# Two decays of a recurrent state moved to VectorE, a matmul narrowed, and a new instruction order in a fused RWKV-6 and hard-swish kernel

## The chip, the cores and the metric

The kernel runs on one core of a Trainium2 chip. The metric is the device time of one execution in microseconds, as the median of several runs. The engines are named as the profile names them: PE is TensorE (PEld its weight loads), DVE is VectorE, ACT is ScalarE, POOL is GpSimd, SP is the engine whose queue issues nearly all transfers.

## What is computed

A recurrence over 768 steps for 4 sequences and 8 heads of width 48, then a feed-forward layer on its output, all in float32:

```python
for t in range(S):                                   # r, k, v, w: (4, 8, 768, 48); u: (8, 48)
    cur = einsum('bhd,bhe->bhde', u[None] * kt, vt)
    y[:, :, t] = einsum('bhd,bhde->bhe', rt, state + cur)
    state = wt[:, :, :, None] * state + einsum('bhd,bhe->bhde', kt, vt)
x = y.transpose(0, 2, 1, 3).reshape(3072, 384)
h = x @ w_in                                         # (384, 2048)
g = h * clip(h + 3, 0, 6) / 6
out = g @ w_out                                      # (2048, 384)
```

## The kernel before

The 3072 tokens are cut into 24 chunks of 128, six per sequence, and two sequences are worked in turn. Chunk `i` goes through these steps. `load_feat` brings its r, k and w. `back_scan` (L430, L434) and `fore_scan` (L439) are products of the decays over half a chunk, backward and forward, on DVE. `make_k` (L450) and `make_r` (L454) scale k and r with them, on DVE for the first seven chunks (`EARLY = 7`) and on POOL after that. `own` (L466, L467, on POOL from chunk 9) and `own_sum` (L483, DVE) give the term with u. `score` (L500) multiplies scaled k by scaled r on PE, and `above` (L507, DVE) copies the part above the diagonal out of PSUM, which frees two PSUM banks. `turn_k` (L516) transposes k, `write` (L600) forms what the chunk adds to the state, and `written` (L611, ACT) copies that out. The state is then carried on by four steps of one small instruction each, on tiles of 112x192 numbers: `decay` (L529: old state times the decay of the first half chunk), `middle` (L537: plus what that half adds), `decay_middle` (L529: times the decay of the second half), `new_state` (L545: plus what the second half adds). Both decays go through the helper `decayed`, so both have line L529; they run on DVE up to chunk 6 and on POOL from chunk 7 on. `read_state` (L578) and `read_values` (L587) give the chunk's output, and `leave` (L685, ACT) copies it to the tile `xT` that feeds the feed-forward layer. A sixth of the rows of `xT` is moved into place by `last_pair` (L692), transfers from SBUF to SBUF of three issues each on SP's queue, four of them for a block.

From chunk 4 on, the PE work of a chunk is one step, `read(i)`: read the state, a short matmul `mark` (L622), `score(i+1)`, another `mark`, `write(i+1)`, read the values, `turn_k(i+2)`. The matmuls of 64 or fewer rows and columns in it use a quarter of the array each, and four of them run at a time; the mark uses one quarter.

Four chunks make a block of 512 tokens; there are six. Block 0 takes the layer in the plain way (L718 up, L729 gate on DVE, L737 down). Blocks 1 to 5 take it by sums and fewer products: DVE first forms sums of the parts of x (`sum_x`, called tx, L780 to L784, written to the tile `T_`), PE runs 40 up products (L833) that leave 7 chains of sums in PSUM banks, DVE and ACT read these out (L850, L848, L841), ACT clips (L854), DVE multiplies (L858, the gate) and forms sums of gated values (`sum_g`, L873), and PE runs 28 down steps of eight products (L888), which ACT and DVE take out (L906, L908). Sums of the weights (`sum_w`, `sum_out`) are made once on DVE by the same lines L780 to L784 and L809. DVE also converts the weights at the start (L413, L417) and later reads inputs a second time to test their range (`vet`, L936 and L943).

One table sets the order of everything. Each step is added to a `Plan` with its engine, a cost in microseconds, the steps that it needs and the buffers that it holds. The string `ORDER` gives the rank of every step, two characters each; the steps are emitted in that rank, and each engine executes its own share of that sequence strictly in that order. The costs of the steps don't change this order when the program is built. They serve the search that made the string, which is not part of the kernel, and they set where `emit` puts idle products (`spin`, L1269) on PE in the first 60 us.

```python
rank = [CODE.index(ORDER[2 * i]) * 64 + CODE.index(ORDER[2 * i + 1]) for i in range(len(steps))]
```

Of the kernel before, what the change touches and what calls it, by code (L numbers as in the profile page):

```python
# [8 lines left out]
F32 = mybir.dt.float32  # L9
# [12 lines left out]
HL = L // 2  # L22
# [59 lines left out]
    "AAADAHAQAKAOAMANAPARASAYAWAjAUAXAaAeAmAqAgAoAzA3A/ACAFATAiAbAnAdAZAcAfAhAlAuAyAkApAxA1A5A9A8A+BOBUBeAJALBGBfBRBZBSBD"  # L82
    "BJBTBVBYCGCLBoBwCBCRBbCYCfCnCwC7AVAwBiB4BuCABzBdBgBlBmBqCSCaCJCOCWCrCNCuC1E1DBDMDVDfBPBQCpC3DdDkCvCUCbCiDDDXDuDyC+DG"
    "DiFCDLFGFKFcFZFnCXDKC9DHEPEbDCDADQDWDsEKFgDZDqFmE6FsFvF+FzF/HgHLCcC4D+EJFpFtEDDYDwD9FfFlF8FkGFF9GVGfGiGlGsDoGSETFjGD"
    "GJEXEEFJFRF6GLG0GBGoGbGvG4HBG+HHHSHVEdF2FwF7GpG1FyGHGIGWGtGzHYGqHPG9HUHcH2HtH4FxG5F1GUGwHEHaGrGQGYHQHjH5HIINHkITIYIw"
    "I4JHL3KhGOHJGRHCHlH0H6HZGkHXH+IOJIIDKPJzK/LELJLbHKKIHOHoIqJCJEIPHmH8KxKyLOKzLKKtLXLeLmL8MHMIHbLTHhJTJeLVLdJZIJIbLULa"
    "LxLgLsL0MNL9MtJLJfJOJtLRLqLzKOJ4LFLuL+MQLtMaNANnOYOeQBOqK3L2LCLiL1MFMJLrLMMBMDMiOkNhObM/OzO4PJPVPgLfOpL4MAMyOZOsMnM9"
    "NIO1PFPeOcPiPBPmPoQJPyP2QTQZM5PcM6NdOrPbPfNpNQOCPkPrP+PlQNPsQPQUQWQcQxNtOlNuPXPqP9QAPhO5PIQIQOQlP1QsQqRSRVR/R2TPTzUG"
    "OwQjOxPxQVQrQuP0PSQRQwRySGRBSSRdSsS2ThTsUJQkTZQ+Q2RRSFSvQ/RURmS5TOT0TQTwToT1UDUPUMUQUoUTRbSQRcSLTnT8UBS7RtSNT5UKUhT9"
    "UXUEUZUkU/U2WYSATySCTqTvUSUjTrTaTuUnU0U6UmVaUlVrXGXfXnXsYIYETYURTxUOUpVOVzUWUyU+XQXmXwVMXpVyXuXzX3YAVQVRVUVeWHXqXvVh"  # L90
    "VxW5XtX1X/XyX4X6X+YDYKYNYRYSBCABAEArAvAsA2AGA4A7AtBAAIBEBIA6BNBBB1B9B7CFCDClCoCmCyA0CTCZBrChBLCHCKCQC6CVC0C5DNDSD7Eh"
    "ElEgEsDPDzD2D1EcCgD/EBDREmCsDgDjDpDvEoE/FDE+FMEHErEuExE4E0FSFVFPFeDtE2E5EpFABHBMBWB3B8B/EUEaEiBaBhBtBjBxB0GCGZGaBcBk"
    "BpBnCCCPEAEIELBFBKBXBsByB2EFEOESB6CECIEeEnEvBvB5B+EwFTFXCMCdCjEMEREWCeCtCzEQEVEYC2C/DEFBFUFhC8DJDOEjEtEzCkCxDFD0D6EC"
    "CqDbDhEZEfEkDIDUDaGEGGGNDTDeDmE3E9FEDlDxD3EqEyE7DcDnDrD4EGENE8FIFNFWFiFqFrFuGAKYF5GKGPGTGXGcGhGnGuJPGxGyG2G6HAHFHGHN"
    "HRI+HTHdHfHiHpHrHxHzIHKuD5D8FFFHFLFOFQFYFbFdFoF3GMGdGgGjGmG3G7G/HDHMHWHeHnHqHuHwH1H3H/IBIEIKIUIXIeIiIlIvI0I6FaF0F4Ge"
    "G8IxJcLAHsHvICIVISIcIsI2JGIdIkItIQIRIhHyIIIFH9IaIpJAI3JDIWIfIZH7IyILIjIrIMIGI7IzIgImIuJFI/JKJUJ5KDJNJlI5I9IoI1JmJuJo"
    "JxJBJSInI8JRJgJyKAKbJrJ/KNJWJiJ2JJJVJhJQJbJpJ7JvKBJaJnJ0JMJ+JqJwKLJYJXKTKcJkJ8JsKEJ1KKKeKfKmKGKQKlKpKFKHKaKiKMKSKRKW"
    "J6J9KjK6KsK7KqLIK2K9KJKrKoKwLpLyK1K5K8LBLDLNLSLYK0K4K+MCLGLPLcMgLoLHLlLWLjLLLkLnL/KCKULQLhKgKkLZLwL6MLMEMGMRMVKZLvL7"
    "KnMTMMMeNvMjMPMSMUMlMkMsM3NMNaM1M+NPMoM0NFMWMcMqMXMuM4NLNGNRMmMxM2MYNEMwM7NHMfMpNSNUMzNVNCNNNJNWNsNwN0NKNON+N/NiNyNf"
    "NgN9ODNbNqNDNXNZNrOIOROgN4N8OKNzN2OBNYNlNkNTNmOHOaOQOhNjN5N6NeOLN3N7OENxNcOTONN1OFOJOiOVOmOtO0O3OdOjOfO2OOOSOUOXOuOv"  # L100
    "OPOWOAOGOMPWPAPLO7PMPHPPOnO8OyPCPTQFPGPNPQPRPaPdPpPtPEPKPOQgPUPnPuRCSBPYP6P3QKPZP4P5QCOoO6PjPvO+O/P7P/QQQbQLQMQaQnO9"
    "QDQEPDQhQSQvSESDQeQmQ3Q7Q0RDRLRWR6RERJRQQyRFRXQiQzQ5Q1RNRgRuR0SHQ8RHRPQtRORIRKRMQ6RARsRaRYReRqRxR5SISMSmSpR+SORhRkR4"
    "R7R3R8SaSjRTRrSTSYSKSWShStS0SdSlTESJSVSfRfRoRlRnRwR9SgSUSqSRSZSXRiSoRpSbS/RzRvSwTGR1SkSPSuSeSxS+TFTLSnSrTNTRSzS3S6TA"
    "S4S8TDTHScSiTBTMTTTfTSTiTcTjSyTUTKTWUaUdTbTeTgTlTmT3UAUCTXTdTkUzTpT6ULWBUxTtT+T7UIT2UiUNUgS1S9T4T/TITJUHUUUfUrUcUqUt"
    "U5TCUeUVTVU1UsVBWCVVUwU3U9VIVJVXVoV4WNWgWkWtVTVWVgU4U8VEVDVKVcV0VmV5VLVZVdU7VwVNV8WpVCVFWIXAVPVpViV2VqV7WrW1W7WRWTXB"
    "XHVvWKW0W9V/WGXCXIVjVsV1WFWVWbWhWoWuXSV+WEWWVGVfVYVnV3V9WMWLWfWAWPWJVSWXVbWSW8VkVuWcXWV6WdWDWZWQWiWjXJXLWmWsXZXbWwWx"
    "XNXUWnWqXOXTWOWUX2X9YJYPX5YQYLYVXKXgX8YBXkXxYMYOYTYYYWYXYaYeXiYCYUX0YfYZYjYlYmWeXMW6XcWyW4W/XVWlW2WvW+XFXXXDXEXoXrXY"
    "XaXhXjW3XPXRXdX7XeXlYGYHYFYnYbYcYhY3YkYuY6ZEZUYpY1Y/ZgZqZ2YdYoYvYgYtY4ZFY+ZKYsYxZyYiZBYyYzY2YrYqZJZCYwaQY8ZIZAZNZXZa"
    "ZoZGZQZTZWaXaZZYZjZsZzY7ZHaHaNY0Y9ZMZZZuZeZhZ0Z+aBaSZLZbZVZOZfZpZvZwZ6Y5ZDaKZPZRZcZiZnZdZSZkZ5ZlabZrZ7Z1Z9Z/aCaEaDaO"
    "Z8aAaeapZmZxaRaYZ3Z4aiarZtaJaIacaLavaaahaGaMaFaTaUadaVafagakama0a/bDaPaWalajaqa8bIanbKbTbLaoa7awa5axa6a4bCatauasaza1"  # L110
    "a3a2a+bEbJbFbGbNbPaybAbBa9bObHbQbMbRbSbUIAJdKdKvJjJ3KVKXMZMdL5MKMOMbMrM8NBNoMhMvPwPzP8QHQXQfQGQYQdQoQpQ9Q4RZRGRjUuVA"
    "UFUYUbUvVHVlVtWaWzbV"
# [132 lines left out]
def fast_path(tc, feat, tok, wflat, ub, ug, moe_w_in, moe_w_out, out, flag, n_chunks):  # L245
# [22 lines left out]
    with ExitStack() as ctx:  # L268
# [175 lines left out]
        def early(i):  # L444
            return nc.vector if i < EARLY else nc.gpsimd
# [85 lines left out]
        def decay(i):  # L531
            new_S(i)
            decayed(early(i), i, 0, states[i % 2])
# [87 lines left out]
        def mark():  # L621
            nc.tensor.matmul(pp.tile([HL, HL], F32, name="ps"), lhsT=ident[HL:, HL:], rhs=ident[HL:, HL:], start=True, stop=True)  # L622
# [378 lines left out]
        for i in range(NT):  # L1001
# [12 lines left out]
            plan.add(f"back{i}", "DVE", 1.40, do(back_scan, i), [f"feat{i}"] + [f"fore{i - 2}"] * (i > 1) + [f"back{i - 1}"] * (i > 0), k,  # L1014
                     [("E", [f"K{i}", f"least{i}"])], port=True)
            plan.add(f"K{i}", "DVE" if dve else "POOL", 0.59 if dve else 1.15, do(make_k, i), [f"back{i}", f"least{i}"] + [f"K{i - 1}"] * (i > 0) + ["later"] * (i == 0),
# [3 lines left out]
            plan.add(f"R{i}", "DVE" if dve else "POOL", 0.6 if dve else 1.15, do(make_r, i), [f"fore{i}"], k + 0.3,  # L1020
                     port=True)
            plan.add(f"least{i}", "ACT", 0.12, do(least, i), [f"back{i}"], k + 0.2)
            if i < BY_PE:
                plan.add(f"own{i}", "DVE", 0.6, do(own, i), [f"feat{i}"] + ["later"] * (i == 0) + [f"own{i - 1}"] * (i > 0), k + OWN,
                         [("rk", [f"dot{i}"])], port=True)
                plan.add(f"dot{i}", "PE", 0.56, do(own_dot, i), [f"own{i}"], k + OWN, [("ps", [f"sum{i}"])])
                plan.add(f"sum{i}", "ACT", 0.12, do(own_sum, i), [f"dot{i}"], k + OWN, [("dg", [f"diag1{i}"])])
            else:
                plan.add(f"own{i}", "POOL", 2.2, do(own, i), [f"rkt{i}", "u"] + [f"own{i - 1}"] * (i > 0), k + 0.4,
                         [("rk", [f"sum{i}"])], port=True)  # L1030
                plan.add(f"sum{i}", "DVE", 0.45, do(own_sum, i), [f"own{i}"], k + 0.5, [("dg", [f"diag1{i}"])])
# [26 lines left out]
            if not last:  # L1058
                plan.add(f"state{i}", "DVE", 0.27, do(new_state, i), [f"decb{i}"] + [f"decay{j}" for j in (i - 2,) if j >= 0 and not is_first(j)],
                         t + 0.5, port=True)  # L1060
# [15 lines left out]
            else:  # L1076
                uses = [f"up{bk}.{d}.{r}" for d in range(2) for r in range(20) if X_PLACE[r][0] == "w"] + [f"tx{bk}.{x}" for x in range(4)]
                space = [("x", uses)] * (c == 0)
                needs, us = [f"decb{i}", f"above{i}"], 1.24
# [33 lines left out]
        for f in range(NFC):  # L1113
            for c0, c1 in parts_of[f]:
# [6 lines left out]
                plan.add(f"gate{n_}", "DVE", 0.07 + 0.134 * m, do(gate, f, c0, c1),  # L1121
# [15 lines left out]
        for d in range(2):  # L1137
            for w_ in range(len(W_SUMS)):
# [11 lines left out]
                plan.add(f"sin{d}.{w_}", "DVE", 0.34, do(sum_w, w_, d), before, SUMS[0] + (w_ + 21 * d) * SUMS[1], hold, port=True)  # L1150
        for n_, (t_, x) in enumerate((t_, x) for t_ in (1, 2, 4, 3) for x in range(2)):
# [5 lines left out]
            plan.add(f"sout{t_}.{x}", "DVE", 0.86, do(sum_out, t_, x), before, SUMS[2] + n_ * SUMS[1],  # L1157
# [5 lines left out]
        for bk in range(NB):  # L1163
            K = BASE[bk]
            moves = [f"move{bk}.{p}.{g}" for p in range(2) for g in range(2)]
            for x in range(4 * (bk > 0)):
                plan.add(f"tx{bk}.{x}", "DVE", 0.335 * (X_PARTS[x + 1] - X_PARTS[x]), do(sum_x, bk, x),
# [3 lines left out]
            for d in range(2 * (bk > 0)):  # L1171
# [39 lines left out]
                for x in range(8):  # L1211
                    plan.add(f"clip{bk}.{d}.{x}", "ACT", 0.625, do(up_ramp, bk, d, x), [r + FINAL[x]], at + 0.866 * due[FINAL[x]] + GATE,
                             [("clip", [f"gate{bk}.{d}.{x}"])])
                    plan.add(f"gate{bk}.{d}.{x}", "DVE", 0.6, do(up_gate, bk, d, x), [f"clip{bk}.{d}.{x}"], at + 0.866 * due[FINAL[x]] + GATE,
                             port=True)
            for p in range(2 * (bk > 0)):
# [401 lines left out]
```

## Time and profile before

| what | value |
|---|---|
| median of 3 runs | 541.25 us (540.81 to 542.64) |
| the profiled execution | 542.08 us, of which the span from first to last instruction is 540.2 us |
| PE busy | 530.0 us, 98% of the span |
| DVE busy | 416.6 us, 77% |
| ACT busy | 263.5 us, 49% |
| POOL busy | 110.2 us, 20% |
| granted PE clock | full in all 40 slices |

PE is busy nearly all the time, so its idle time and the products that do no work are what an order can take away. The other engines' shares are averages over very different stages: DVE is busy nine tenths and more in most slices of the first 90 us and of 135 to 200 us, and mostly three to eight tenths later. A matmul record lasts longer than the step to the next one, since matmuls overlap.

### The profile page before, as it was taken

To read this page: it belongs to the slowest core of one execution; us is meant where nothing else is said; L and a number is where in the kernel's file an instruction comes from. 1 tells how busy PE (TensorE), PEld (TensorE's weight loads), DVE (VectorE), ACT (ScalarE), POOL (GpSimd) and SP (SyncE) were. 2 spreads that over 40 slices of the span, in tenths; PEclk is the share of its full clock that TensorE was granted. 3 is DMA by queue.
4 is the path that set the end of the run, shared out by engine and by line. 5 is a ranking of instruction groups with operands and counts; after the bars stand their busy time and mean duration, and the time that the engine had idled before them with its cause. 6 is when DMAs were issued, how large, how long until landed. Compare 5 with 4: busy or idle time off the path is not lost. (4 is left out here: it accounts for less than half of the span.)

```text
span 540.2 us, 13522 instructions
## 1 busy us (share of the span) xinstructions
PE 530.0 (98%) x5626; PEld 470.1 (87%) x5626; DVE 416.6 (77%) x709; ACT 263.5 (49%) x657; POOL 110.2 (20%) x111
## 2 busy tenths in 40 slices
PE   8999999999999999999999999999999999999997
PEld 8887877666788999888889988899988999988997
DVE  8999999675999996889787888967768845358651
ACT  5999795252555434446434354635254435253400
POOL 2000003742422054111332341303350001000000
PEclk9999999999999999999999999999999999999999
DMA  8948653333234434733205785002630001100001
GB/s 341 368 160 312 237 177 105 116 106 105 74 115 151 139 94 164 250 133 130 95 17 193 256 282 205 1 10 92 208 134 1 0 2 36 41 1 1 8 8 47
DMA packets 21458, 66.42 MB, mean 123 GB/s; under 512 B 3312, under 2 KB 11408, under 8 KB 21392
## 3 DMA queue, kind: packets, MB, share of 16 engines
q1 hardware_dynamic: 21264, 65.50, 35.3%
q8 instruction: 46, 0.75, 0.5%
q14 instruction: 20, 0.16, 0.1%
q10 hardware_dynamic: 128, 0.00, 0.0%
HBM read 59.69 MB, written 4.72 MB: 119 GB/s over the span
## 5 line engine op out<-in xcount | busy, mean ns | idle before, releaser
L854 ACT ACTIVATE clip<-g,three 128x512 f32<-128x512 f32 x80 | 56.3, 720 | 55.0 <-DVE g L850 38.9
L850 DVE TENSOR_TENSOR g<-bank,g 128x512 f32<-128x512 f32 x80 | 53.4, 681 | 16.0 <-PE bank L833 15.1
L858 DVE SCALAR_TENSOR_TENSOR g<-clip,g 128x512 f32<-128x512 f32 x80 | 57.9, 740 | 6.1 <-ACT clip L854 5.9
L888 PE MATMUL bank<-w_out,g 128*128 128x192 f32 x320 | 57.3, 328 | 1.0 <-DVE g L858 1.0
L888 PEld LDWEIGHTS bank<-w_out,g 128*128 128x128 f32 x320 | 52.5, 190 | 2.5 <-DVE g L858 1.5
L491 ACT ACTIVATE A<-eyes,dg 128x64 f32<-128x64 f32 x192 | 50.4, 339 | 6.6 <-PE y_ps L587 6.3
L450 POOL TENSOR_TENSOR K<-feat_in,E 112x512 f32<-112x512 f32 x17 | 24.4, 1433 | 121.4 <-PE ps L622 117.7
L454 POOL TENSOR_TENSOR W<-feat_in,W 112x512 f32<-112x512 f32 x17 | 22.3, 1312 | 116.7 <-DVE W L439 108.9
L718 PE MATMUL bank<-xT,w_in 128*128 128x256 f32 (+1 forms) x216 | 45.2, 361 | 0.0
L685 ACT COPY xT<-y_ps 48x256 f32<-48x256 f32 x88 | 32.1, 365 | 24.8 <-PE y_ps L587 23.9
L737 PE MATMUL bank<-w_out,g 128*128 128x384 f32 x128 | 43.2, 488 | 0.0
L833 PE MATMUL bank<-xT,w_in 128*128 128x256 f32 x160 | 40.9, 381 | 0.8 <-DVE g L850 0.7
L718 PEld LDWEIGHTS bank<-xT,w_in 128*128 128x128 f32 x216 | 36.7, 190 | 4.7
L848 ACT COPY g<-bank 128x512 f32<-128x512 f32 x50 | 28.9, 582 | 21.5 <-PE bank L833 21.3
L737 PEld LDWEIGHTS bank<-w_out,g 128*128 128x128 f32 x128 | 23.8, 190 | 14.5
L439 DVE TENSOR_TENSOR_SCAN W<-feat_in,start 112x520 f32<-112x520 f32 x24 | 29.6, 1234 | 8.6 <-PE y_ps L578 8.6
L833 PEld LDWEIGHTS bank<-xT,w_in 128*128 128x128 f32 x160 | 30.0, 190 | 5.9 <-DVE g L850 2.1
L430 DVE TENSOR_TENSOR_SCAN E<-feat_in,back 112x520 f32<-112x520 f32 x24 | 32.5, 1354 | 2.9 <-DMA feat_in<-in_feat_dram 1.3
L841 ACT ACTIVATE bankS<-bank 128x512 f32<-128x512 f32 x20 | 11.6, 582 | 40.4 <-PE bank L833 31.9
L833 PE MATMUL bank<-xT,bits 128*128 128x256 f32 x120 | 30.7, 381 | 0.0
L888 PE MATMUL bankS<-w_out,g 128*128 128x192 f32 x160 | 28.8, 326 | 0.0
L888 PE MATMUL bank<-more,g 128*128 128x192 f32 x160 | 28.1, 326 | 0.0
(291 smaller groups left out, 1136.7 us busy)
## 6 DMA issues: line engine op xcount, KB each, us to landing
feat_in<-in_feat_dram SPq DMA_DIRECT2D x23, 772.5 KB, 4.8
bits<-in_moe_w_in_dram SPq DMA_DIRECT2D x8, 768.0 KB, 5.4
bits<-in_moe_w_out_dram SPq DMA_DIRECT2D x8, 768.0 KB, 5.7
feat_in<-in_moe_w_in_dram SPq DMA_DIRECT2D x8, 768.0 KB, 4.8
feat_in<-in_moe_w_out_dram SPq DMA_DIRECT2D x8, 768.0 KB, 4.6
rk_in<-in_tok_dram SPq DMA_DIRECT2D x15, 384.0 KB, 5.1
v_in<-in_tok_dram SPq DMA_DIRECT2D x24, 192.0 KB, 4.5
feat_in<-in_wflat_dram SPq DMA_DIRECT2D x6, 768.0 KB, 4.6
```

What stands on the lines that cost most here:

```text
L430: nc.vector.tensor_tensor_scan(out=E_[:, ::-1], data0=d["w"][:, :0:-1], data1=back.rearrange("q p t -> q (p t)")[:, ::-1], initial=0.0, op ...
L439: nc.vector.tensor_tensor_scan(out=W_, data0=d["w"][:, :-1], data1=starts[i % 2].rearrange("q p t -> q (p t)"), initial=0.0, op0=ALU.mult, ...
L491: nc.scalar.activation(out=d["A"][:, h, :], in_=eyes, func=ACT.Copy, scale=d["dg"][:, h])
L685: nc.scalar.copy(out=blocks[bk]["xT"][g * GP:g * GP + D, :, at:at + HL], in_=st[i]["y_ps"][a][(g ^ a) * GP:(g ^ a) * GP + D, :, :])
L718: nc.tensor.matmul(h_ps[:, :(c1 - c0) * L], lhsT=w_in[:, f // 2, j, f % 2, :], rhs=b["xT"][:, j, c0 * L:c1 * L], start=(j == 0), stop=(j = ...
L737: nc.tensor.matmul(b["o", c][:, :DM], lhsT=g_of(0, f, c), rhs=w_out[:, f, :], start=(f == 0), stop=(f == NFC - 1))
L833: nc.tensor.matmul(b["p", d, c][:, z * HB:(z + 1) * HB], lhsT=weight(W_PLACE[r], d)[:, z, :], rhs=x_at(bk, X_PLACE[r]), start=fresh and z ...
L848: nc.scalar.copy(out=out_, in_=src)
L850: nc.vector.tensor_tensor(out=out_, in0=src, in1=out_of(bk, d, other), op=ALU.add if sign > 0 else ALU.subtract)
L854: nc.scalar.activation(out=c, in_=out_of(bk, d, u), func=ACT.Relu, bias=three, scale=twice)
L858: nc.vector.scalar_tensor_tensor(out=g, in0=blocks[bk]["r", d, u], scalar=6.0, in1=g, op0=ALU.min, op1=ALU.mult)
L888: nc.tensor.matmul(b["d", p, to][:, :h], lhsT=a, rhs=w(), start=(f == 0 and k in (1, 5)), stop=(f == HF - 1 and k in (2, 3, 4)), skip_grou ...
```

## The change

Four things change together.

1. `decay` and `decay_middle` call the helper with `nc.vector` for every chunk. From chunk 7 on, that is 15 and 17 instructions that go from POOL to DVE. In the plan the first is listed on DVE; the second is still listed on POOL with its old cost, though the instruction is DVE's.
2. `mark` multiplies by 4 columns of the identity instead of 64. There are 38 marks.
3. The costs of about a dozen kinds of step are raised in the plan (DVE's sums, scans and gates, POOL's products).
4. The string `ORDER` is a new one, 1750 ranks.

```diff
         def decay(i):
             new_S(i)
-            decayed(early(i), i, 0, states[i % 2])
+            decayed(nc.vector, i, 0, states[i % 2])
...
             if is_first(i):
                 new_S(i)
-            decayed(early(i), i, 1, st[i]["kvs"][:, 0] if is_first(i) else st[i]["S"][:, 1])
+            decayed(nc.vector, i, 1, st[i]["kvs"][:, 0] if is_first(i) else st[i]["S"][:, 1])
...
         def mark():
-            nc.tensor.matmul(pp.tile([HL, HL], F32, name="ps"), lhsT=ident[HL:, HL:], rhs=ident[HL:, HL:], start=True, stop=True)
+            nc.tensor.matmul(pp.tile([HL, 4], F32, name="ps"), lhsT=ident[HL:, HL:], rhs=ident[HL:, :4], start=True, stop=True)
...
-                plan.add(f"decay{i}", "DVE" if dve else "POOL", 0.27 if dve else 0.9, do(decay, i),
+                plan.add(f"decay{i}", "DVE", 0.33, do(decay, i),
...
-                plan.add(f"tx{bk}.{x}", "DVE", 0.335 * (X_PARTS[x + 1] - X_PARTS[x]), do(sum_x, bk, x),
+                plan.add(f"tx{bk}.{x}", "DVE", 0.46 * (X_PARTS[x + 1] - X_PARTS[x]), do(sum_x, bk, x),
```

The new order at three places. The first is PE's, where block 1 takes over from block 0, from the end of `read(8)` on. L737 are the last down products of block 0, L833 the first up products of block 1; `T__1817` and `T__1789` are the same tile of sums of x before and after. Before:

```order
L587 MATMUL y_ps<-A,v_in 48x64 x16
L516 MATMUL ps<-ident,K 128x112 x4
L737 MATMUL bank<-w_out,g_861 128x384 x2
L833 MATMUL bank<-T__1817,bits 128x256 x2
L737 MATMUL bank<-w_out,g_861 128x384 x2
L833 MATMUL bank<-T__1817,w_in 128x256 x2
L833 MATMUL bankS<-T__1817,w_in 128x256 x2
```

Now:

```order
L587 MATMUL y_ps<-A,v_in 48x64 x16
L516 MATMUL ps<-ident,K 128x112 x4
L737 MATMUL bank<-w_out,g_478 128x384 x6
L833 MATMUL bank<-T__1789,bits 128x256 x2
L737 MATMUL bank<-w_out,g_863 128x384 x8
L833 MATMUL bank<-T__1789,w_in 128x256 x2
```

Between the read and the second up product PE now has 14 down products of block 0 where it had 4.

The second place is SP's queue ahead of block 1. L692 are the moves into `xT`, three issues each; L352 is a chunk's r, k and w, L364 and L369 its other inputs, L925 data for a vet. Before:

```order
L364 DMA v_in<-in_tok_dram 128x384 x3
L352 DMA feat_in<-in_feat_dram 128x1545
L692 DMA xT<-xT 16x256 x3
L369 DMA rk_in<-in_tok_dram 128x768
L692 DMA xT<-xT 16x256 x6
L352 DMA feat_in<-in_feat_dram 128x1545
L692 DMA xT<-xT 16x256 x3
L369 DMA rk_in<-in_tok_dram 128x768
```

Now:

```order
L692 DMA xT<-xT 16x256 x3
L352 DMA feat_in<-in_feat_dram 128x1545
L369 DMA rk_in<-in_tok_dram 128x768
L352 DMA feat_in<-in_feat_dram 128x1545
L364 DMA v_in<-in_tok_dram 128x384
L369 DMA rk_in<-in_tok_dram 128x768
L692 DMA xT<-xT 16x256 x3
L352 DMA feat_in<-in_feat_dram 128x1545
L692 DMA xT<-xT 16x256 x6
L364 DMA v_in<-in_tok_dram 128x384
```

One of the four moves goes out two chunk loads earlier; the last two still stand behind the load of chunk 12.

The third place is DVE's, at the same time as the first: the sums of x for block 1 (L780 to L784 on `T_`), then the forward scan, the state and the copy that frees the banks of `score(9)`. Before:

```order
L780 SCALAR_TENSOR_TENSOR T__1817<-xT 128x256
L780 SCALAR_TENSOR_TENSOR T__1817<-xT,T__1817 128x256
L782 TENSOR_TENSOR T__1817<-T__1817,xT 128x256
L780 SCALAR_TENSOR_TENSOR T__1817<-xT,T__1817 128x256
L784 TENSOR_TENSOR bits<-w_in 128x2x128
L784 TENSOR_TENSOR T__1817<-xT 128x256
L784 TENSOR_TENSOR T__1817<-T__1817 128x256
L782 TENSOR_TENSOR T__1817<-T__1817,xT 128x256
L784 TENSOR_TENSOR bits<-w_in,bits 128x2x128
L439 SCALAR_TENSOR_TENSOR W<-feat_in,start_79 112x520
L784 TENSOR_TENSOR bits<-w_in,bits 128x2x128
L545 TENSOR_TENSOR state_81<-S,kvs 112x192
```

Now:

```order
L780 SCALAR_TENSOR_TENSOR T__1789<-xT,T__1789 128x256
L784 TENSOR_TENSOR bits<-w_in 128x2x128
L439 SCALAR_TENSOR_TENSOR W<-feat_in,start_79 112x520
L784 TENSOR_TENSOR bits<-bits,w_in 128x2x128
L545 TENSOR_TENSOR state_81<-S,kvs 112x192
L483 TENSOR_REDUCE dg<-rk 128x8
L507 COPY_PREDICATED A<-mask,bank 128x4x64 x2
L784 TENSOR_TENSOR bits<-w_in 128x2x128
L784 TENSOR_TENSOR T__1789<-xT 128x256
L784 TENSOR_TENSOR T__1789<-T__1789 128x256
L782 TENSOR_TENSOR T__1789<-T__1789,xT 128x256
L529 TENSOR_TENSOR S<-state_82,w_min 112x192
```

The scan, the state and the copy L507 now come right after the first four sums of x, ahead of the next three, and a decay (L529) stands in DVE's queue.

More of the change, by code (lines that the diff above doesn't have):

```diff
@@ L86 @@
[L86 to L90, printed above, removed]
@@ L1058, in fast_path @@
             if not last:
[L1059 removed]
+                plan.add(f"state{i}", "DVE", 0.35, do(new_state, i), [f"decb{i}"] + [f"decay{j}" for j in (i - 2,) if j >= 0 and not is_first(j)],
                          t + 0.5, port=True)
```

85 lines of the change are left out of this document (45 added, 40 removed).

## The prediction

> **What bounds the kernel now.** I began with the page's head. The first row is the span, the second the engines' shares of it.
>
> ```profile
> span 540.2 us, 13522 instructions
> PE 530.0 (98%) x5626; PEld 470.1 (87%) x5626; DVE 416.6 (77%) x709; ACT 263.5 (49%) x657; POOL 110.2 (20%) x111
> ```
>
> PE leaves 10.2 us of the span idle, and all its needed products stay. So the order can win only PE's idle time, or products that do nothing. Next I read PE's timeline for places where PE waited after the start. In each row stand the start, the duration, the work, and in brackets the idle time before it with what ended it.
>
> ```profile
> 136.44 0.48 PE L833 MATMUL bank<-T__1817,w_in 128*128 128x256 f32 x1 [1.16 <-DVE A L507]
> 168.30 0.48 PE L833 MATMUL bank<-xT,w_in 128*128 128x256 f32 x1 [0.42 <-DVE g L850]
> 181.30 0.40 PE L888 MATMUL bank<-bits,S__2285 128*128 128x192 f32 x1 [0.19 <-DVE S__2285 L873]
> ...
> 237.68 0.48 PE L833 MATMUL bank<-T__2742,bits 128*128 128x256 f32 x1 [0.72 <-DVE g L850]
> 264.72 0.43 PE L888 MATMUL bank<-w_out,g 128*128 128x192 f32 x1 [1.02 <-DVE g L858]
> 273.20 0.40 PE L888 MATMUL bank<-w_out,S__2970 128*128 128x192 f32 x1 [0.41 <-ACT o L906]
> 275.12 0.43 PE L888 MATMUL bank<-w_out,S__2970 128*128 128x192 f32 x1 [0.38 <-DVE S__2970 L873]
> 346.64 0.48 PE L833 MATMUL bank<-xT,w_in 128*128 128x256 f32 x1 [0.28 <-DVE g L850]
> ```
>
> Seven of the eight end on DVE. They sum to 4.58 us. Each costs more than its idle time, because the matmul before it runs out unaccompanied. The page's group and the chain of waits give the size.
>
> ```profile
> L888 PE MATMUL bank<-w_out,g 128*128 128x192 f32 x320 | 57.3, 328 | 1.0 <-DVE g L858 1.0
> 363.50 7.82 PE bank L888 x48
> ```
>
> One record lasts 328 ns, but 48 in a row take 7.82 us, 0.163 us each, so a restart adds about 0.165 us. Eight waits cost 4.58 + 8 x 0.165 = 5.9 us: 2.3 us for the first three, 3.6 us for the other five. That is nearly all that an order can win after the start.
>
> The first three have one origin. The windows give the busy time of PE, PEld, DVE, ACT and POOL in a stretch; the timeline rows below them show DVE, PE, then SP's queue.
>
> ```profile
> 120.00:130.00 10.00, 10.00 (x95) 6.01 (x94) 4.38 (x8) 1.54 (x6) 2.94 (x3) 1.00 0.61 194
> 130.00:137.00 7.00, 5.84 (x101) 4.20 (x93) 6.90 (x15) 3.52 (x10) 1.28 (x1) 1.00 0.14 16
> 137.00:182.00 45.00, 44.22 (x319) 38.05 (x318) 44.86 (x71) 23.87 (x50) 12.48 (x10) 1.00 0.35 115
> ```
>
> ```profile
> 129.37 0.43 DVE L780 SCALAR_TENSOR_TENSOR T__1817<-xT 128x256 f32<-128x256 f32 x1 [5.00 <-DMA rk_in<-in_tok_dram]
> ...
> 134.36 1.34 DVE L545 TENSOR_TENSOR state<-S,kvs 112x192 f32<-112x192 f32 x1
> ...
> 116.01 13.08 PE L737 MATMUL bank<-w_out,g 128*128 128x384 f32 x40
> ...
> 124.34 1.77 SPq L692 DMA_DIRECT2D xT<-xT  x3
> ```
>
> DVE idles 5.00 us at the first sum of x for block 1. The row names another transfer, but this sum reads `xT`, and the last move into it was issued from 124.34 on. From 129.37 DVE has no pause: 44.86 of the next 45 us. The read of chunk 8, the sums, a scan, a state and the copy L507 queue up behind, and PE, which has only four down products and one up product in between, waits at 136.44. The waits at 168.30 and 181.30 lie in the same unbroken stretch.
>
> **The marks: 0 us.** Three groups by form bound this.
>
> ```profile
> L475 PE MATMUL ps<-u_col,rk 112*64 112x2 f32 x144 | 5.7, 200 | 0.3 <-DVE rk L463 0.3
> L622 PE MATMUL ps<-ident 64*64 64x64 f32 x76 | 10.5, 217 | 0.0
> L1269 PE MATMUL bankS<-ident 128*128 128x128 f32 x68 | 11.4, 320 | 1.4 <-POOL ident masks.py:199 1.4
> ```
>
> A matmul with 64 weight columns lasts 217 ns with 64 moving columns and 200 ns with two. If all of that difference were on PE's path, 76 records would give 76 x 17 ns = 1.3 us. I take 0, since a mark fills one quarter of the array while three others work, and the weight load is the same; bounds 0 to -1.3 us. The Trainium skill's page "TensorE: Matmul & The Clock Gate", section "Back-to-back issue gap", gives an isolated gap of N/2.4 + 2.5 ns with a floor of about 25 ns up to 64 columns; as an estimate 29 against 25 ns, so 76 x 4 ns = 0.3 us, and the total would be 0.3 us less; no run here shows that floor.
>
> The plan now places 36 idle products where it had 34. One costs 11.4/34 = 0.34 us, two at most 0.7 us. They stand in the first 60 us where PE waits on DVE anyway, so I take 0, bounds 0 to +0.7.
>
> **The decays.** Groups by form, DVE's rows first, then POOL's:
>
> ```profile
> L537 DVE TENSOR_TENSOR S<-S,kvs 112x192 f32<-112x192 f32 x20 | 11.4, 570 | 6.6 <-ACT kvs L611 6.6
> L529 DVE TENSOR_TENSOR S<-state,w_min 112x192 f32<-112x192 f32 x5 | 2.1, 415 | 0.0
> L529 DVE TENSOR_TENSOR S<-S,w_min 112x192 f32<-112x192 f32 x5 | 1.7, 346 | 0.0
> ...
> L529 POOL TENSOR_TENSOR S<-state,w_min 112x192 f32<-112x192 f32 x15 | 13.9, 929 | 0.3 <-DVE state L545 0.3
> L529 POOL TENSOR_TENSOR S<-S,w_min 112x192 f32<-112x192 f32 x15 | 11.6, 775 | 50.9 <-DVE S L537 47.0 <-DMA feat_in<-in_moe_w_in_dram 3.9
> ```
>
> DVE gains 32 x 0.346 = 11.1 us in its queue, and POOL loses about 27 of 110 us (two more decays at the second row's price). Beside its 124 us of idle time DVE can carry that; what matters is where. But POOL's work also costs DVE time:
>
> ```profile
> 262.11 2.56 DVE L858 SCALAR_TENSOR_TENSOR g<-clip,g 128x512 f32<-128x512 f32 x2
> ...
> 262.27 0.89 POOL L529 TENSOR_TENSOR S<-S,w_min 112x192 f32<-112x192 f32 x1 [3.70 <-DVE S L537]
> 263.13 0.99 POOL L466 TENSOR_TENSOR rk<-rk_in 128x384 f32<-128x384 f32 x1
> ```
>
> Two gates take 2.56 us here, against 0.69 us alone (DVE's row at 261.24 below), while POOL runs a decay and a product; PE's 1.02 us wait at 264.72 ends on the second gate. The 1.34 us at 134.36 is the same thing: the instruction has the shape of the 346 ns row.
>
> ```profile
> 261.24 0.69 DVE L858 SCALAR_TENSOR_TENSOR g<-clip,g 128x512 f32<-128x512 f32 x1
> ```
>
> So a quarter of POOL's work less should take about a quarter of these collisions away.
>
> **The order, first group: -2.3 us.** From the read of chunk 8 to that of chunk 10, PE gets ten more down products. Forty records took 13.08 us, so a product (two records) takes 0.654 us, ten give 6.5 us. DVE's queue between the same reads grows by five decays (1.7 us) and two sums of weights and loses one vet:
>
> ```profile
> L936 DVE TENSOR_REDUCE w_max<-feat_in 128x1 f32<-128x1536 f32 x6 | 10.5, 1742 | 1.1 <-DMA feat_in<-in_wflat_dram 1.1
> L784 DVE TENSOR_TENSOR bits<-w_in,bits 128x256 f32<-128x256 f32 x4 | 1.6, 412 | 0.0
> ```
>
> That is 1.7 + 0.8 - 1.7 = +0.8 us, against 6.5 us more cover. The copy L507 that ended the longest wait has five instructions ahead of it in DVE's queue after the read, where it had nine, and PE runs fourteen down products and one up product in between instead of four and one; so the 1.16 us wait has more than 5 us of reserve. Three of the twelve moves leave SP two chunk loads earlier. The last six still stand behind the load of chunk 12, which waits for POOL's product of chunk 9 (L454); their issue alone takes 2 x 1.77 = 3.5 us, so the first sum may still pause, and up to 5 us of it would be covered. If that cover were gone, the 2.3 us would be back.
>
> **The second group: -0.9 us.** The five later waits (3.6 us) come from single collisions and late gates, at places that the new order mixes anew. Between 0 (others take their place) and -3.6 (none is left) I take a quarter, for the quarter of POOL's work. Sum: 0 + 0 - 2.3 - 0.9 = -3.2 us. The profiled execution took 542.08 us and would take 538.9. It stood 0.8 us above the median, so the median goes from 541.25 to **538.1 us**.
>
> **The rivals.** *All waits go*: 541.25 - 5.9 = 535.3 us. For it speaks that seven of eight waits end on one engine, whose lateness has a few origins; against it, that collisions with POOL remain, 83 us of POOL's work.
>
> *The waits only move*: new order, as many waits at other places, 541.2 us. For it speaks that eight small waits are spread over 210 us and that DVE now has 11 us more to do; against it, the 6.5 us of cover at the worst place.
>
> *DVE overflows*, the case on the other side. The place is DVE's queue from the sums of x for block 1 on. If the six moves behind the load of chunk 12 land more than 6 us late, DVE has its 5.0 us pause again, and from there it has no idle time (44.86 of 45 us), so the five decays go straight to PE: +1.7 us. In the next stretch that was full,
>
> ```profile
> 240.00:260.00 20.00, 20.00 (x202) 17.09 (x201) 19.50 (x31) 12.73 (x25) 2.86 (x2) 1.00 0.28 91
> ```
>
> three more cost 1.0 us; with the two idle products at 0.34 us it is 541.25 + 3.4 = 544.6 us. It decides once DVE's idle time between the two reads is used up. The Trainium skill's page "SBUF — State Buffer", section "Who interferes with whom", speaks for it: a VectorE instruction with two inputs in SBUF contends with a GpSimd instruction that reads SBUF, and the loser blocks for the whole instruction; the moved decays have two such inputs. The trace agrees: the five decays of old states on DVE average 415 ns, against 346.
>
> *The marks count*: with the 1.3 us in full, 536.8 us.
>
> **How the numbers follow.** I give the forecast 0.48 with a range of its own from 536.5 to 539.6, marks that count 0.06, all waits gone 0.10, waits that only move 0.20, DVE's overflow 0.16. This kernel can tell 0.3% (1.6 us) from no change: faster is below 539.6, slower above 542.9. The first three cases give 0.64 faster, the fourth 0.20, the last 0.16. The range for 8 in 10 runs from 535.2 (all waits gone) to 542.4, which leaves out the overflow and a little below.
>
> **What would show it.** Right: no wait of PE between the block's first L833 and 182 us above 0.3 us, DVE's pause before the first sum of x below 2 us, L529 on DVE 44 times near 0.35 us, PE's idle time down from 10.2 to about 7.5 us. The marks are right if the steps of a read keep their length. Wrong: a pause of 4 us or more at a first sum of x, or new waits of PE on L850 or L858 above 3.6 us in all after 182 us; then DVE was the bound at more places than I saw.

## The result and the profile after

The changed kernel takes 535.32 us (median of four runs, 535.13 to 536.49); the kernel before took 541.94 us beside it. The ratio is 0.9881, with a 95% interval from 0.9863 to 0.9900, so 6.4 us are gone (5.4 to 7.4). The forecast was 3.2 us. The profiled execution took 535.24 us. The page's head:

```profile
span 533.3 us, 13527 instructions
...
PE 527.5 (99%) x5630; PEld 471.5 (88%) x5630; DVE 421.9 (79%) x741; ACT 263.8 (49%) x657; POOL 88.7 (17%) x79
```

PE now leaves 5.8 us of the span idle instead of 10.2. What is left is in the list of PE's waits (line waiting, what ended the wait, us in all, times, longest):

```profile
PE bankS L1269 <- POOL ident masks.py:199: 1.4, 1, 1.4
PE bank L888 <- DVE S__2969 L873: 0.3, 1, 0.3
PE ps L475 <- DVE rk L463: 0.3, 1, 0.3
PE bank L718 <- DVE w_in L417: 0.2, 1, 0.2
```

Three of the four lie in the first 60 us. The fourth stands at 268.98 (0.32 us), where the eight waits after the start had 4.58 us before; beside it there is a gap of about 0.1 us at 171.94 that is not in this list. Both groups went but for that, so the case *all waits go* (535.3 us) is the one that came nearest.

At the place of the first group the timeline reads as follows: SP's queue, DVE, then PE.

```profile
113.77 0.33 SPq L352 DMA_DIRECT2D feat_in<-in_feat_dram  x1
114.20 3.67 SPq L692 DMA_DIRECT2D xT<-xT  x6
...
119.15 0.43 DVE L780 SCALAR_TENSOR_TENSOR T__1789<-xT 128x256 f32<-128x256 f32 x1 [0.25 <-issue]
...
125.88 4.05 PE L737 MATMUL bank<-w_out,g 128*128 128x384 f32 x12
...
130.63 5.32 PE L737 MATMUL bank<-w_out,g 128*128 128x384 f32 x16
135.79 1.03 PE L833 MATMUL bank<-T__1789,w_in 128*128 128x256 f32 x4
```

The load of chunk 12 is issued at 113.77 where it was issued at 123.77, the last six transfers into `xT` follow at once, and the first sum of x starts at 119.15 after a pause of 0.25 us. PE runs its 28 records of down products and never waits.

Groups by form, for the parts that moved:

```profile
L529 DVE TENSOR_TENSOR S<-S,w_min 112x192 f32<-112x192 f32 x20 | 7.8, 391 | 0.1
L537 DVE TENSOR_TENSOR S<-S,kvs 112x192 f32<-112x192 f32 x20 | 9.6, 478 | 3.1 <-ACT kvs L611 3.1
L622 PE MATMUL ps<-ident 64*64 64x4 f32 x76 | 8.6, 182 | 0.0
```

The decays on DVE cost about 390 ns on the mean, not 346. L537 fell from 570 to 478 ns. A mark's record fell from 217 to 182 ns.

### The profile page after: what moved, and what is told of

Its sections match the earlier page's. It is cut to its first block, busy times and chain, and to the rows that moved or that the text cites. A ratio compares the mean times of both kernels' runs of the same rounds, so it can differ in the third digit from the quotient of the medians.

```text
span 533.3 us, 13527 instructions
## 1 busy us (share of the span) xinstructions
PE 527.5 (99%) x5630; PEld 471.5 (88%) x5630; DVE 421.9 (79%) x741; ACT 263.8 (49%) x657; POOL 88.7 (17%) x79
## 4 chain that ended last, share of the span: by engine, by line
PE 93%; DVE 4%; issue 1%; ACT 1%; DMA 1%; DVEq 0%; ACTq 0%
PE bank L888 29%; PE bank L833 25%; PE bank L737 8%; PE bank L718 7%; PE bankS L888 5%; PE bankS L833 4%; PE y_ps L578 3%; PE y_ps L587 2%; PE bank L500 2%; PE ps L516 2%; PE y_ps L600 2%; PE bankS L1269 1%; PE ps L475 1%; DVE g L858 1%; DVE g L850 1%
## 5 line engine op out<-in xcount | busy, mean ns | idle before, releaser
L850 DVE TENSOR_TENSOR g<-bank,g 128x512 f32<-128x512 f32 x80 | 54.1, 685 | 22.3 <-PE bank L833 21.2
L450 POOL TENSOR_TENSOR K<-feat_in,E 112x512 f32<-112x512 f32 x17 | 24.9, 1466 | 175.0 <-PE ps L622 150.1
L454 POOL TENSOR_TENSOR W<-feat_in,W 112x512 f32<-112x512 f32 x17 | 22.8, 1341 | 125.7 <-DVE W L439 125.7
L737 PE MATMUL bank<-w_out,g 128*128 128x384 f32 x128 | 43.4, 488 | 0.0
L833 PE MATMUL bank<-xT,w_in 128*128 128x256 f32 x160 | 40.5, 380 | 0.1
L906 ACT ACTIVATE o<-bank 128x192 f32<-128x192 f32 x30 | 9.5, 329 | 56.2 <-PE bank L888 56.1
L737 PEld LDWEIGHTS bank<-w_out,g 128*128 128x128 f32 x128 | 23.8, 190 | 14.3 <-DVE w_out L417 0.2
L833 PEld LDWEIGHTS bank<-xT,w_in 128*128 128x128 f32 x160 | 30.2, 190 | 4.4 <-DVE g L850 0.5
L430 DVE TENSOR_TENSOR_SCAN E<-feat_in,back 112x520 f32<-112x520 f32 x24 | 30.2, 1258 | 1.2 <-DMA feat_in<-in_feat_dram 1.1
L833 PE MATMUL bank<-xT,bits 128*128 128x256 f32 x120 | 30.4, 380 | 0.0
L466 POOL TENSOR_TENSOR rk<-rk_in 128x384 f32<-128x384 f32 x15 | 21.0, 1402 | 46.4 <-DVE dg L483 29.2
```

Source lines behind the costliest of these rows:

```text
L430: nc.vector.tensor_tensor_scan(out=E_[:, ::-1], data0=d["w"][:, :0:-1], data1=back.rearrange("q p t -> q (p t)")[:, ::-1], initial=0.0, op ...
L737: nc.tensor.matmul(b["o", c][:, :DM], lhsT=g_of(0, f, c), rhs=w_out[:, f, :], start=(f == 0), stop=(f == NFC - 1))
L833: nc.tensor.matmul(b["p", d, c][:, z * HB:(z + 1) * HB], lhsT=weight(W_PLACE[r], d)[:, z, :], rhs=x_at(bk, X_PLACE[r]), start=fresh and z ...
L850: nc.vector.tensor_tensor(out=out_, in0=src, in1=out_of(bk, d, other), op=ALU.add if sign > 0 else ALU.subtract)
```

## The experiments

The question is which part of the change paid, and why the second group of waits, of which the forecast took only a quarter, went nearly whole. All ratios are to the kernel before, run beside each on the same chip.

### The marks alone, and the changed kernel without them

```diff
-            nc.tensor.matmul(pp.tile([HL, HL], F32, name="ps"), lhsT=ident[HL:, HL:], rhs=ident[HL:, HL:], start=True, stop=True)
+            nc.tensor.matmul(pp.tile([HL, 4], F32, name="ps"), lhsT=ident[HL:, HL:], rhs=ident[HL:, :4], start=True, stop=True)
```

> Only the marks are cut from 64 to 4 columns; decays and order as before. Theory (the prediction's term): a mark fills one quarter of the array while three others work, so 0 us, ratio 0.999 to 1.001, and the steps of a read keep their length although the record itself may get shorter. Rival: the shorter record counts on PE's path, 76 x 17 ns = 1.3 us, ratio 0.9976.

Measured: 0.9985 (0.9974 to 0.9997), that is 0.8 us, between the two expectations. The steps of a read do not get shorter. Here are the first and the last step of the same read, first in the kernel before, then with the marks alone:

```profile
277.91 0.67 PE L578 MATMUL y_ps<-W,S 48*48 48x64 f32 x32
...
280.11 0.60 PE L516 MATMUL ps<-ident,K 112*128 112x112 f32 x4
```

```profile
276.61 0.67 PE L578 MATMUL y_ps<-W,S 48*48 48x64 f32 x32
...
278.81 0.60 PE L516 MATMUL ps<-ident,K 112*128 112x112 f32 x4
```

From the start of the first to the start of the last both take 2.20 us. What differs is waits: the one at 136 us is 0.83 instead of 1.16 us, and the one at 237.68 (0.72 us) is missing. After the first of these places the reads lie 0.3 us earlier than in the kernel before, after the second 1.3 us, and that distance then stays to PE's last products (532.99 instead of 534.29): no read in between gets shorter. The wait at 237.68 is missing in the profiles of the decays alone, of the early moves and of the later products below too, all of which have the old order there. It goes with a transfer: in the kernel before, DVE stands 2.54 us at a range test (L943, at 232.01) until its data has landed, and the readouts that PE waits for come after it; in those four profiles DVE stands there 0 to 1.70 us. So the kernel before probably has this wait in some executions only. As a second test of the marks they were put back into the changed kernel, with the reverse of the diff above:

> The changed kernel with marks of 64 columns again; order and decays stay. Theory (marks 0 us, and the 0.8 us that the marks alone brought in the kernel before came through one of its small waits, which the new order has no more): ratio to the kernel before as for the changed kernel, 0.987 to 0.9895. Rival (76 shorter records are worth about 0.8 us on PE's path wherever they stand): 0.99 to 0.991.

Measured: 0.9863 (0.9840 to 0.9886), median 535.66 us. The interval holds the changed kernel's 0.9881 and leaves out the rival's 0.99 and more. In the new order the marks are worth nothing that can be measured; in the old one the interval allows up to 1.4 us, and the profile shows that only as smaller waits.

### The decays alone, and the order alone

Decays alone, marks and order as before:

```diff
-            decayed(early(i), i, 0, states[i % 2])
+            decayed(nc.vector, i, 0, states[i % 2])
...
-            decayed(early(i), i, 1, st[i]["kvs"][:, 0] if is_first(i) else st[i]["S"][:, 1])
+            decayed(nc.vector, i, 1, st[i]["kvs"][:, 0] if is_first(i) else st[i]["S"][:, 1])
```

> Only the decays of chunks 7 on move from GpSimd to VectorE, in the order of before. Theory A (the second group of waits came from GpSimd's work beside VectorE's): the five later waits of PE (3.6 us) go for the most part, the first three stay, as the pause of 5 us before the first sum of x stays and VectorE's queue behind it gets 1.7 us longer; in all 539 to 541 us against 541.9, ratio 0.995 to 0.999. Theory B (the second group went through the new order): in the old order 11 us more on VectorE go to PE where VectorE was full; first waits +1.7 us, second group as large or larger, 543 to 546 us, ratio 1.002 to 1.008.

Order alone, where only the string is exchanged:

```diff
-    "AAADAHAQAKAOAMANAPARASAYAWAjAUAXAaAeAmAqAgAoAzA3A/ACAFATAiAbAnAdAZAcAfAhAlAuAyAkApAxA1A5A9A8A+BOBUBeAJALBGBfBRBZBSBD"
+    "AAADAHAQAKAOALANAPARASAYAWAjAUAXAaAeAmAqAfAoAzA3A/ACAFATAiAbAnAdAZAcAgAhAlAuAyAkApAxA1A5A9A8A+BOBUBdAJAMBGBfBRBZBSBD"
...
```

> Only the table of the order is new; decays stay on GpSimd and marks have 64 columns. Theory A: the first group of waits goes (-2.3 us), the second stays, since GpSimd still works beside VectorE: 539 to 540 us, ratio 0.995 to 0.997. Theory B: both groups go with the order, 535.5 to 536.5 us, ratio 0.988 to 0.990, and the decays are worth nothing. A third reading: the order was made for decays that take 0.33 us on VectorE; at 0.8 to 0.9 us on GpSimd states come late and new waits of PE on L873 or L545 appear, ratio near 1.

Measured: the decays 0.9995 (0.9980 to 1.0010), the order 0.9882 (0.9863 to 0.9902). The order alone is the whole gain; theory B gave 535.5 to 536.5 us, and the median is 535.17. The decays alone are worth nothing that can be measured, so neither theory on them holds: they do remove one wait, others come, and the first three waits don't grow in sum (0.71, 0.64 and 0.20 us, against 1.16, 0.42 and 0.19). The two gates that took 2.56 us take 1.30, and PE passes 264 us without a wait. But these remain, or are new, in the timeline of the decays alone:

```profile
261.48 1.30 DVE L858 SCALAR_TENSOR_TENSOR g<-clip,g 128x512 f32<-128x512 f32 x2
...
271.30 1.54 PE L888 MATMUL bank<-w_out,S__2970 128*128 128x192 f32 x8 [0.41 <-ACT o L906]
273.22 1.57 PE L888 MATMUL bank<-w_out,S__2970 128*128 128x192 f32 x8 [0.38 <-DVE S__2970 L873]
302.96 1.13 PE L833 MATMUL bank<-T__3586,bits 128*128 128x256 f32 x4 [0.45 <-DVE o L908]
...
340.16 1.13 PE L833 MATMUL bank<-xT,bits 128*128 128x256 f32 x4 [0.54 <-ACT g L848]
```

With the order alone, POOL still does all its decays, and the collisions are still there, but on other work. DVE first, then POOL, then PE:

```profile
259.44 1.48 DVE L873 TENSOR_TENSOR S__2967<-S__2967,g 128x512 f32<-128x512 f32 x1
260.84 0.68 DVE L858 SCALAR_TENSOR_TENSOR g<-clip,g 128x512 f32<-128x512 f32 x1
...
257.64 1.32 POOL L466 TENSOR_TENSOR rk<-rk_in 128x384 f32<-128x384 f32 x1 [1.74 <-issue]
259.04 1.33 POOL L467 TENSOR_TENSOR rk<-rk,u_bc 128x384 f32<-128x384 f32 x1
...
262.98 1.46 PE L888 MATMUL bank<-bits,S__2967 128*128 128x192 f32 x8
```

POOL's two products now meet two sums (at 258.03 and 259.44), which take 1.48 us each instead of 0.68; PE takes the next product on that sum tile at 262.98, 2 us after the second one's end. The last gate meets nothing and takes 0.68 us. In the changed kernel the same place looks different again: there it is POOL that is held up. Its product lasts 4.27 us, and the two sums take 0.68 us each:

```profile
257.70 4.27 POOL L466 TENSOR_TENSOR rk<-rk_in 128x384 f32<-128x384 f32 x1 [2.38 <-issue]
```

### The order in two halves

The old and the new table can be joined at about 220 us, between the two groups of waits: there the first 800 steps of the one are followed by all others in the order of the other. Marks and decays are as before.

```diff
-ORDER = all steps in the old order
+ORDER = the first 800 steps of the new order, then the rest in the old order
```

> Marks and decays as before. The program's steps up to the middle of block 1 (about 220 us) stand in the new order, the rest in the old one. Theory (each half's gain comes from its own half): the waits at 136, 168 and 181 us go (2.3 us), those on L850, L858, L906 and L873 after 220 us stay at their old distance from the reads; 539 to 540 us against 542.2, ratio 0.994 to 0.997. Rival (a better start lets all later work run ahead of PE, so the second half profits too): the later waits shrink as well, below half of their 2.8 us of idle time, ratio 0.989 to 0.992.

And the other way round:

```diff
-ORDER = all steps in the old order
+ORDER = the first 800 steps of the old order, then the rest in the new order
```

> The other half: old order up to about 220 us, new order from there; marks and decays as before. Theory: the first three waits stay as they were, the five later ones (3.6 us) go although all decays are still on GpSimd, 538.5 to 539.5 us, ratio 0.992 to 0.995; with the half above the two gains add up to the 6.4 us of the whole order. Rival (as above): the later half alone gives less than half of that, ratio above 0.996.

Measured: 0.9953 (0.9936 to 0.9970) and 0.9931 (0.9910 to 0.9953). Their product is 0.9884, against 0.9882 for the whole order. So, as far as these intervals tell, the gains simply add: 2.5 us for the new front, 3.7 us for the new back. The lists of waits show which stay in each (without those of the first 60 us), first with the new front,

```profile
PE bank L888 <- DVE g L858: 1.0, 1, 1.0
PE bank L833 <- DVE g L850: 0.5, 2, 0.3
PE bank L888 <- ACT o L906: 0.4, 1, 0.4
PE bank L888 <- DVE S__2970 L873: 0.4, 1, 0.4
PE bank L833 <- ACT g L848: 0.2, 1, 0.2
```

then with the new back:

```profile
PE bank L833 <- DVE A L507: 1.1, 1, 1.1
PE bank L833 <- DVE g L850: 0.4, 1, 0.4
PE bank L888 <- DVE S__2968 L873: 0.3, 1, 0.3
PE bank L888 <- DVE S__2285 L873: 0.2, 1, 0.2
```

With the new front the wait on L507 and the one at 181 us are gone, and the one at 168 us stands at 172.06 with 0.26 us (half of the list's L850). With the new back the first three stay, and among the later ones a single wait is left, of 0.27 us at 271.58.

### The moves into xT early, and late

First the kernel before, with all four moves ahead of the load of chunk 12: two of them ahead of the token load of chunk 10, the other two behind the load of r, k and w of chunk 11.

```diff
-        out = [n for _, n in sorted(zip(rank, steps))]
+        out = [n for _, n in sorted(zip(rank, steps))]; [out.insert(out.index(at), out.pop(out.index(n))) for n, at in (("move1.0.0", "tok10"), ("move1.0.1", "tok10"), ("move1.1.0", "rkt11"), ("move1.1.1", "rkt11"))]
```

> The kernel before with one thing moved on the transfer queue: the first four moves into xT for block 1 are issued ahead of the loads of chunks 10 and 11, so that the first sum of x no longer stands behind the load of chunk 12. Theory (the three first waits have one origin, VectorE's pause of 5.00 us at the first sum of x): the pause falls below 1 us, the waits at 136, 168 and 181 us go (2.3 us), ratio 0.995 to 0.997. Rival (PE has only four down products and one up product there, and VectorE's queue is what it is): the pause goes, but the waits stay above half of their 1.8 us of idle time, ratio 0.998 to 1.001.

Measured: 0.9968 (0.9954 to 0.9982), 1.7 us. SP's queue shows where the moves had stood. In the kernel before, then with the early moves:

```profile
96.65 19.35 SPq L364 DMA_DIRECT2D v_in<-in_tok_dram  x3
```

```profile
97.32 10.13 SPq L364 DMA_DIRECT2D v_in<-in_tok_dram  x2
107.56 4.46 SPq L692 DMA_DIRECT2D xT<-xT  x6
```

The queue stood for 19 us at the token loads of chunks 7, 9 and 10, whose three buffers are freed by PE's reads; everything behind them was late, the load of chunk 12 included. With two moves ahead of the last of these loads and two soon behind it, DVE has no pause at the first sum, and PE starts the product that had waited 1.16 us without a wait. But the other two waits stay:

```profile
135.77 1.03 PE L833 MATMUL bank<-T__1817,w_in 128*128 128x256 f32 x4
...
167.16 1.13 PE L833 MATMUL bank<-xT,w_in 128*128 128x256 f32 x4 [0.42 <-DVE g L850]
...
180.17 1.54 PE L888 MATMUL bank<-bits,S__2285 128*128 128x192 f32 x8 [0.20 <-DVE S__2285 L873]
```

So the theory holds for the longest wait alone. That wait with its restart is 1.3 us, and the measured 1.7 us (1.0 to 2.5) asks for no more; the ratio by itself would have passed for the whole theory.

Then the changed kernel, with its two early moves put behind the load of chunk 12, so that all twelve transfers stand there. (In the kernel before, only three of the twelve stood behind that load; in the changed kernel six do.)

```diff
-        out = [n for _, n in sorted(zip(rank, steps))]
+        out = [n for _, n in sorted(zip(rank, steps))]; [out.insert(out.index("feat12") + 1, out.pop(out.index(n))) for n in ("move1.0.1", "move1.0.0")]
```

> The changed kernel, with the two moves into xT that it issues ahead of the load of chunk 12 put behind that load, as in the kernel before (all twelve transfers then go out from about 114 us on, 7 us of issuing). Theory (the prediction's: a pause up to 5 us is covered by the ten down products): VectorE pauses 1 to 4 us before the first sum of x, PE shows no new wait above 0.3 us, ratio to the kernel before 0.987 to 0.990 as for the changed kernel. Rival (VectorE has no reserve behind that sum): the pause goes through to PE, waits of 1 us and more at L833 near 130 us, ratio 0.991 to 0.995.

Measured: 0.9889 (0.9866 to 0.9912), as for the changed kernel. SP, DVE and PE:

```profile
114.00 7.46 SPq L692 DMA_DIRECT2D xT<-xT  x12
...
122.78 0.43 DVE L780 SCALAR_TENSOR_TENSOR T__1789<-xT 128x256 f32<-128x256 f32 x1 [4.08 <-DMA xT<-xT]
...
143.00 1.13 PE L833 MATMUL bank<-T__1789,bits 128*128 128x256 f32 x4 [0.34 <-DVE g L850]
```

DVE pauses 4.08 us, where it paused 5.00 us in the kernel before, and PE waits 0.34 us in all of the next 20 us, just over the 0.3 us of the theory. So the new order covers the pause. The run doesn't separate its two covers: the ten more down products on PE, and the copy L507 that comes earlier in DVE's queue.

### Two of POOL's products moved

To test the collisions by themselves, the kernel before got only this: the products L466 and L467 of chunk 17 run behind the decay of chunk 15, those of chunk 18 some 12 us later.

```diff
-        out = [n for _, n in sorted(zip(rank, steps))]
+        out = [n for _, n in sorted(zip(rank, steps))]; [out.insert(out.index(at) - 1, out.pop(out.index(n))) for n, at in (("own17", "sum17"), ("own18", "R17"))]
```

> The kernel before with two products of GpSimd moved (L466, L467 of chunks 17 and 18): the first behind the decay of chunk 15, the second to the end of the read of chunk 15's neighbour, about 281 us. In the profile before they lie beside VectorE's last gates (two in 2.56 us) and beside the sums L873 (1.49 and 1.48 us). Theory (these waits are single collisions between the two engines): the gates and sums take 0.7 us each, the waits at 264.72 (1.02 us) and 275.12 (0.38 us) go, the one on ACT L906 at 273.20 stays; with two restarts 1.7 us, ratio 0.996 to 0.998. Rival (as the run with the decays alone suggests, where the wait at 264.72 went and others came): the two waits go and the products collide with something else that PE waits for, ratio 0.999 to 1.001.

Measured: 0.9960 (0.9943 to 0.9976), 2.2 us. DVE, then PE:

```profile
262.11 2.08 DVE L858 SCALAR_TENSOR_TENSOR g<-clip,g 128x512 f32<-128x512 f32 x2
...
271.69 0.68 DVE L873 TENSOR_TENSOR g<-g 128x512 f32<-128x512 f32 x1
...
264.24 1.57 PE L888 MATMUL bank<-w_out,g 128*128 128x192 f32 x8 [0.55 <-DVE g L858]
...
272.15 2.76 PE L888 MATMUL bank<-w_out,S__2970 128*128 128x192 f32 x16
```

The sums fall to 0.68 us, and the wait of 0.38 us goes, as expected. The gates still meet two decays and take 2.08 us, so the wait there is halved, not removed. The wait put down to ACT (L906) goes too, which the expectation had wrong. The moved products of chunk 17 now meet the first sums behind the gates, of which the second takes 1.48 us (at 265.52) in place of 0.99, and PE doesn't wait for it. Moving four of POOL's instructions thus brings 2.2 us (1.3 to 3.1) where the whole back half of the new order brings 3.7. The waits that went come to 1.3 us with two restarts on top, 1.6 us; a wait of 0.38 us at 217.68 (DVE's L908), ahead of the moved products, is in this profile and not in the one before.

### Twice more decays on DVE

Last, how much room DVE has in the new order. In the changed kernel the decay of the old state is issued three times from chunk 7 on, with the same result.

```diff
-            decayed(nc.vector, i, 0, states[i % 2])
+            [decayed(nc.vector, i, 0, states[i % 2]) for _ in range(3 if i >= 7 else 1)]
```

> The changed kernel, with the decay of an old state issued three times in a row for each of the chunks 7 on (same result): 15 to 17 chunks x 2 x 0.39 us = 12 to 13 us more on VectorE, as much again as the change itself put there. Theory (VectorE has reserve where the decays stand, since the order leaves PE's inputs ready in time): 0 to +1 us over the changed kernel, ratio to the kernel before 0.988 to 0.990. Rival (the last of the reserve is used up, the overflow of the prediction): a fifth to a half of the added time reaches PE, +2.5 to +6 us, ratio 0.993 to 0.999.

Measured: 0.9936 (0.9913 to 0.9958), about 3.0 us slower than the changed kernel: the rival. L529 has 30 more instructions, and DVE's busy time rises from 421.9 to 440.0 us, more than the 12 to 13 us expected. One place carries the largest part of the 3.0 us, a wait of 1.23 us and a restart. POOL, DVE, then PE:

```profile
227.92 1.54 POOL L466 TENSOR_TENSOR rk<-rk_in 128x384 f32<-128x384 f32 x1 [8.81 <-DVE dg L483]
229.54 1.00 POOL L467 TENSOR_TENSOR rk<-rk,u_bc 128x384 f32<-128x384 f32 x1
230.50 1.29 POOL L450 TENSOR_TENSOR K<-feat_in,E 112x512 f32<-112x512 f32 x1
...
228.52 3.48 DVE L529 TENSOR_TENSOR S<-state,w_min 112x192 f32<-112x192 f32 x3
...
233.26 1.13 PE L833 MATMUL bank<-T__2729,w_in 128*128 128x256 f32 x4 [1.23 <-DVE g L850]
```

Three decays take 3.48 us beside three of POOL's products. In the changed kernel the one decay at this place takes 1.16 us, and PE does not wait; two more do not fit.

```profile
228.27 1.16 DVE L529 TENSOR_TENSOR S<-state,w_min 112x192 f32<-112x192 f32 x1
```

## Why the prediction was right, and where it was wrong

The direction was right, and 535.32 us lies at the lower edge of the range, outside the forecast's own 536.5 to 539.6. The profile of the changed kernel does what was named for "right": no wait of PE above 0.3 us between the block's first L833 and 182 us, a pause of 0.25 us at the first sum, 44 decays on DVE, though at 0.39 us rather than 0.35. PE's idle time fell further than the 7.5 us named, to 5.8.

**The second group is the term that failed.** The prediction said: "Between 0 (others take their place) and -3.6 (none is left) I take a quarter, for the quarter of POOL's work." The back half of the order alone measures 3.7 us (2.5 to 4.9), with every decay still on POOL. Not only the size was off but the reason. The collisions were the right suspect (moving four of POOL's instructions brought 2.2 us), but the amount of POOL's work does not decide: the decays taken off POOL bring nothing that can be measured in the old order and nothing in the new one. For the waits from 264 to 275 us, what decides is which of DVE's instructions a collision falls on. On the last gates before PE needs them, 1.26 us of delay cost PE 1.02 us of waiting; on a sum with 2 us to spare, nothing. The one wait that is left in the changed kernel, at 268.98, ends on such a late sum, of 1.49 us beside POOL's L466. The other two waits were not tested by themselves. The one at 346.64 follows two gates that take 2.73 us beside POOL's L467 and L450, so it looks like a collision as well. The one at 237.68 goes with the transfer for a range test, and in the new order DVE hardly stands at these tests any more. Its idle time ahead of them is behind the last bar of each row, in the kernel before and in the changed one (with the order alone it is 1.1 us):

```profile
L943 DVE SCALAR_TENSOR_TENSOR words<-feat_in,words 128x768 int32<-128x768 int32 x15 | 15.0, 1001 | 5.4 <-DMA feat_in<-in_moe_w_in_dram 5.4
L943 DVE SCALAR_TENSOR_TENSOR words<-feat_in,words 128x768 int32<-128x768 int32 x15 | 15.9, 1061 | 0.0
```

The prediction had written "at places that the new order mixes anew", and then priced that as a share of POOL's work, as if the new places were drawn at random.

**The first group** was sized right: 2.3 us forecast, 2.5 us measured (1.6 to 3.5). Its cover is shown by the late moves, a pause of 4.08 us with one wait of 0.34 us behind it: "up to 5 us of it would be covered" holds for 4.08. One step was wrong on the way, and one was left out. "The first three have one origin" is true of the first alone; with the pause gone, 0.42 us at 167 and 0.20 us at 180 stay. And the six late transfers left a pause of 0.25 us only, because the load of chunk 12 went out 10 us earlier. That it waits for POOL's product L454 of chunk 9 is right for the new order: the product ends at 113.74, and the load goes out at 113.77. But in the kernel before this product ended at 116.70, and the load went out at 123.77. There it was held by SP's queue, which had stood at the token load of chunk 10, and the new order puts that load behind the moves.

**The marks** were right at 0 in the new order. The estimate of 0.3 us beside them took 64 columns by the formula and 4 by the floor; at that floor, which it quotes as holding up to 64 columns, the two would not differ. **The decays** were priced at 346 ns each and took about 390; still DVE's busy time rose by 5.3 us only, not by 11, since L537 got shorter, and the backward scan L430 too (1354 to 1258 ns). That is not for POOL's smaller load alone: with the order alone, where POOL does all its decays, L537 takes 449 ns. **The rivals**: *all waits go* gave 535.3 us, within 0.1 us of the measured time, but that is partly luck. It took 5.9 us off a median of 541.25, where the kernel before took 541.94 beside the changed one and the gain is 6.4; and its 5.9 us hold the wait at 237.68, which is probably not in every execution, while one of 0.32 us stayed. Against this case stood "that collisions with POOL remain, 83 us of POOL's work", which is true and cost no more than that last wait. *DVE overflows* did not happen, but it was not far: twice more decays cost 3.0 us, where the change's own cost none. The Trainium skill's page "SBUF — State Buffer", section "Who interferes with whom", says that a VectorE instruction with two inputs in SBUF contends with a GpSimd instruction that reads SBUF. The three decays in 3.48 us beside POOL's products agree with that; the rule says nothing on whether PE feels it.

**Open** stays which engine's queue in the back half of the order matters most, since PE's, DVE's and ACT's orders depend on each other and were not exchanged one by one; and why the transfer behind the wait at 237.68 lands at different times. Of the 6.9 us by which the profiled span got shorter, 4.4 are PE's idle time and 2.5 its busy time; eight restarts make 1.3 us of the latter by the prediction's estimate, and the rest was not traced.

## What to carry to other kernels

When two engines disturb each other, look first at which instruction each collision hits and how long its result has before it is needed; moving four instructions of the disturbing engine brought 2.2 us, moving a quarter of its work away brought nothing. Price a searched order by the waits that are there, each with its own cause, and not by a share of them: where PE is 98% busy and its waits are small and separate, nearly all of them may go. And for a pause before a late transfer, read the whole transfer queue back to the entry at which it stood, since what waits there need not be what lies just ahead of the transfer.

## What the runs showed of the hardware

A matmul record with 4 moving columns in place of 64 lasts 182 ns in place of 217, but a read that holds four such records takes 2.20 us to the start of its last step either way: in these reads the shorter record gives nothing. A decay on DVE takes 346 ns on the mean of five and 1.16 us beside POOL's products (three in 3.48 us). The one of 1.16 us began 0.94 us before the end of the POOL instruction beside it; its delay of 0.8 us is more than twice its own time and about as long as what was left there. The delay can also fall on POOL: where two sums of DVE take 1.48 us each, the product beside them takes 1.32 us, and where they take 0.68 us each, it takes 4.27.
